# Top-k attention and two mixtures on one core: float64 weights converted by an integer sum, with raw words finished by the casts, later evictions of x, later products of w3, and exponentials written over the scores

## The chip, the core and the metric

One Trainium2 chip (trn2); the kernel runs on one of its cores. The metric is the device time of one execution in microseconds. The matrix engine is called PE (its weight loads PEld), the vector engine DVE, the scalar engine ACT, GpSimd POOL, and the engine that issues the transfers here SP. Each engine works through its own queue in order; an instruction that waits holds up all that stand behind it on the same engine.

## What is computed

Four batches of eight heads, 576 positions, 64 values per head. Each row of scores keeps its 32 largest and is normalised over them; the result x (2304 x 512) passes a first mixture, `(x w1 * x w2) w3 w_out`, and then a second one of eight experts with weights from a few rounds of normalising by rows and columns.

```python
scores = scale * np.matmul(q, k.transpose(0, 1, 3, 2))
kth = np.partition(scores, -top_k, axis=-1)[..., -top_k:-top_k + 1]
scores = np.where(scores >= kth, scores, -1000000000.0)
attn = np.exp(scores - np.max(scores, axis=-1, keepdims=True))
attn = attn / (np.sum(attn, axis=-1, keepdims=True) + 1e-09)
x = np.matmul(attn, v)
...
h = (x @ w1) * (x @ w2) @ w3
x = h @ w_out
...
out += P[:, e:e + 1] * (np.maximum(x @ w1[e], 0.0) @ w2[e])
```

The weights w1, w2, w3 and w_out of the first mixture arrive as float64, eight bytes per number, and the kernel makes float32 of them itself.

## The kernel before

**Attention steps.** The loop of line 615 runs once per step: a step treats two blocks of 128 score rows, and there are 72 steps (0 to 71) and a few more to empty the pipeline. In step s DVE finds the 32 largest of step s's rows (`st_topk`, lines 214 to 229: four rounds of MAX8 for two blocks, with three rounds of MATCH_REPLACE8 between them). In the same step ACT and POOL finish the rows of step s-1 (`st_over`, `st_bias`, `st_exp`: clamp, offset, exponential with its sum), DVE takes the reciprocal of step s-2's sums (`st_rec`, line 255) after its first MAX8, POOL normalises step s-2 (`st_norm`), PE transposes it (`st_trans`) and multiplies it with v (`st_av`), and PE makes the scores of step s+1 (`st_scores`), which ACT evicts. `st_av` ends with ACT's eviction of x (lines 295 and 304). Scores live in `s_sb` (three buffers), exponentials in `e_sb` (two).

**Conversions.** There are 40 pieces of 128x512 numbers (lines 399 to 420): 8 of w_out (key "o"), 16 of w3 (key "3"), 8 of w1, 8 of w2. `cv_run` (line 341) treats a piece in this way. From the top 16 bits of each raw word ACT makes two clamped numbers, `ca` and `cb` (lines 351 and 352). DVE joins them by a minimum and a maximum into the upper half of Q (line 359: the sign, the exponent and the first bits of the result as a float), masks sign and exponent out of Q (line 363) and multiplies the second word of the raw number by that power of two (line 373; for w_out ACT scales the word in line 356 and POOL multiplies in line 371). POOL adds the result to Q (lines 376 and 378). w1 and w2 are then split into a rounded upper part by ACT and a remainder by POOL (`hi_lo`, line 333). The DVE pieces are closures in `dve_q`; `st_topk` takes one after each pair of MAX8 and each pair of MATCH_REPLACE8, seven slots per step (`dve_slot`). `run_cv` is called twice in a step and starts the next piece while no more than three closures stand in the queue. The raw words have three buffers (`RB`), and the load for the piece three places on is issued behind the product (line 374).

**Work fed between.** While the attention steps run, PE is also given items from `fill` by a budget (`run_fill`, line 547). First come w3's transposes and its products with w_out (`w_items`, line 455), 5500 ns per step. When all of w3 is done, the conversion of w2 may begin (line 563, which closes the pools of w_out and w3); when w2 is converted, the first mixture starts (line 619). Its work for a batch has to be done by the step in which the next batch's attention ends (`marks`: steps 19, 37, 55, 73), and the budget of a step is what is left divided by the steps that are left (line 625).

Of the kernel before, what the change touches and what calls it, by code (L numbers as in the profile page):

```python
# [17 lines left out]
def kernel(  # L18
# [258 lines left out]
    def st_av(st):  # L277
# [6 lines left out]
        if steps1[st][0][1] is None:  # L284
# [8 lines left out]
            for j in range(2):  # L293
                b, hp = divmod(steps1[st][j][0], HP)
                nc.scalar.activation(xT[b][:, hp, S4:S], ps[:, 64 * j:64 * j + 64], AF.Copy)
            return
# [19 lines left out]
    gsc = G.rearrange("p f t -> p (f t)")  # L316
    cbias = const.tile([128, 2], F32, name="cbias")
    nc.gpsimd.memset(cbias[:, 0:1], -8.0 * 16 * 896)
    nc.gpsimd.memset(cbias[:, 1:2], -8.0 * (16 * 896 + 32768 - 4096))
    nc.gpsimd.memset(gsc[:, 0:2 * CW], 0.0)  # L320

    def cv_load(key, src):
        t = cv["p"].tile([128, 4 * CW + 4], U16, name="raw", tag="raw", bufs=RB)
# [17 lines left out]
    def cv_run(key, dst, done=None):  # L341
        t = raws.pop(key)
        pos = cpos[0]
        y = t[:, 4:4 * CW + 4].rearrange("p (n f) -> p n f", f=4)[:, :, 0]
        rest = t.bitcast(U32)[:, 0:2 * CW].rearrange("p (n f) -> p n f", f=2)[:, :, 1]
        n, m = cv["n"] % 2, cv["n"] % 3
        cv["n"] += 1
        Q = gsc[:, CW * n:CW * n + CW]
        ca = gsc[:, CW * (2 + m):CW * (3 + m)]
        cb = cv["p"].tile([128, CW], F32, name="cb", tag="cb", bufs=1 if "w2" in m1p else 2)  # L350
        nc.scalar.activation(ca, y, AF.Relu, bias=cbias[:, 0:1], scale=8.0)
        nc.scalar.activation(cb, y, AF.Identity, bias=cbias[:, 1:2], scale=8.0)

        off = key[0] == "o"
        if off:
            nc.scalar.activation(rest.bitcast(F32), rest, AF.Copy, scale=2.0 ** -36)

        def c1():
            nc.vector.scalar_tensor_tensor(Q.bitcast(U16).rearrange("p (n f) -> p n f", f=2)[:, :, 1],  # L359
                                           ca, 32768.0, cb, op0=ALU.min, op1=ALU.max)  # L360

        def c2():
            nc.vector.tensor_scalar(ca.bitcast(U32), Q.bitcast(U32), 0xff800000, None, op0=ALU.bitwise_and)

# [72 lines left out]
    def w_trans(i, hf):  # L437
        if hf == 0:
            w3t[i] = wtp.tile([128, FC, 128], F32, name="w3t", tag="w3t", bufs=1)
# [3 lines left out]
        nc.scalar.activation(w3t[i][:, 4 * hf:4 * hf + 4].rearrange("p a b -> p (a b)"), pt, AF.Copy)  # L443
        w3done.add((i, hf))
# [601 lines left out]
```

## Time and profile before

| | |
|---|---|
| median of three runs | 2446.41 us (2446.24 to 2447.53) |
| span of the profiled execution, first to last instruction | 2442.0 us |
| time of the profiled execution apart from its span | not stated by the profile |
| PE busy | 2288.3 us (94%) |
| DVE busy | 1958.9 us (80%) |
| POOL busy | 1343.2 us (55%) |
| ACT busy | 1256.2 us (51%) |
| attention steps 0 to 71, first MAX8 to last reciprocal | 14.25 to 806.1 us |

How to read it: the shares of a whole span mix stages. The attention steps fill the first third, the second mixture nearly all of the rest. An instruction's time on an engine can overlap the next one's start, so what a piece costs on an engine that never idles is the distance from its start to the next start, not its duration. A row such as "DVE rden L255 <- ACT rden L249: 8.0, 5, 4.1" says that DVE sat idle ahead of line 255 for 8.0 us in 5 cases, the longest 4.1, until ACT's line 249 was done.

### The profile page before, as it was taken

How to read it: one execution, taken by the hardware profiler on the slowest of the kernel's cores; microseconds unless marked ns; L12 is line 12 of the kernel's file. 1: busy time of each engine (PE TensorE's matmuls, PEld its weight loads, DVE VectorE, ACT ScalarE, POOL GpSimd, SP SyncE). 2: the span in 40 equal slices, each digit the busy share in tenths (PEclk: the TensorE clock that was granted, in tenths of full speed). 3: DMA queues.
4: the chain of work that ended last, by engine and by line, in shares of the span. 5: the costliest groups of instructions: out<-in, count | busy, mean ns of one | idle time of the engine just before them, and what ended most of it. 6: DMA issues, size and time to landing. Idle time of an engine off the chain costs nothing.

```text
span 2442.0 us, 37866 instructions
## 1 busy us (share of the span) xinstructions
PE 2288.3 (94%) x13061; PEld 2002.0 (82%) x13061; DVE 1958.9 (80%) x3560; ACT 1256.2 (51%) x2725; POOL 1343.2 (55%) x1377
## 2 busy tenths in 40 slices
PE   4677699899899999999999999999999999999999
PEld 3454489789788888889999988888888899999998
DVE  7998999999999228887777778777777777777776
ACT  6686777777777333444443444443444443444342
POOL 4534443233332125686666668666666666666664
PEclk7898789999999999999999999999999999999999
DMA  4332211111110132222222232222222322222221
GB/s 132 111 97 77 85 35 44 41 45 36 49 32 11 46 116 66 74 82 69 65 67 70 70 100 83 67 63 70 69 69 62 95 70 69 69 63 68 70 70 52
DMA packets 173296, 166.59 MB, mean 68 GB/s; under 512 B 19632, under 2 KB 137392, under 8 KB 173104
## 3 DMA queue, kind: packets, MB, share of 16 engines
q1 hardware_dynamic: 173104, 164.17, 22.4%
q8 instruction: 103, 1.69, 0.3%
q14 instruction: 89, 0.73, 0.1%
HBM read 145.24 MB, written 9.44 MB: 63 GB/s over the span
## 4 chain that ended last, share of the span: by engine, by line
PE 80%; DVE 11%; ACT 5%; POOL 2%; issue 2%; DMA 1%; SPq 0%; POOLq 0%; DVEq 0%; ACTq 0%
PE y L933 31%; PE l1ps L866 27%; PE abps L492 8%; PE x2ps L510 4%; DVE tkv L221 4%; DVE tk L227 3%; PE xps L300 3%; PE sps L198 2%; PE tps L267 2%; PE wps L451 1%; DVE G L359 1%; PE pt L137 1%; ACT e_sb L246 1%; ACT et L270 1%; ACT s_sb L202 1%
## 5 line engine op out<-in xcount | busy, mean ns | idle before, releaser
L730 POOL TENSOR_TENSOR wal<-ws,wah 128x256 fp32r<-128x256 f32 x665 | 553.9, 840 | 482.7 <-ACT wah L729 471.7
L946 DVE SCALAR_TENSOR_TENSOR acc<-y,P,acc 128x512 f32<-128x512 f32 x540 | 402.4, 745 | 215.0 <-PE y L933 214.0
L729 ACT ACTIVATE wah<-ws 128x256 fp32r<-128x256 f32 x672 | 276.3, 413 | 521.2 <-PE l1ps L866 514.9
L933 PE MATMUL y<-wbh,hh 128*128 128x512 f32 x1152 | 456.3, 396 | 4.5 <-ACT hh L887 4.5
L933 PE MATMUL y<-wbl,hh 128*128 128x512 f32 x1152 | 454.6, 395 | 0.0
L933 PE MATMUL y<-wbh,hl 128*128 128x512 f32 x1152 | 449.1, 390 | 1.9 <-DVE hl L890 1.4
L723 DVE TENSOR_TENSOR ws<-ws 128x256 f32<-128x256 f32 x384 | 319.0, 832 | 2.4 <-DMA ws<-in_moe_w_dram 1.8
L221 DVE MAX8 tkv<-tk 128x8 f32<-128x576 f32 x432 | 305.8, 752 | 0.0
L866 PE MATMUL l1ps<-xo0h,wah 128*128 128x384 f32 x896 | 304.6, 340 | 0.0
L866 PE MATMUL l1ps<-xo0h,wal 128*128 128x384 f32 x896 | 302.7, 338 | 0.0
L866 PE MATMUL l1ps<-xo0l,wah 128*128 128x384 f32 x896 | 302.7, 338 | 0.0
L933 PEld LDWEIGHTS y<-wbl,hh 128*128 128x128 f32 x1152 | 216.0, 188 | 52.7
L887 ACT ACTIVATE hh<-u 128x384 fp32r<-128x384 f32 x192 | 100.9, 525 | 297.0 <-DVE u L879 297.0
L933 PEld LDWEIGHTS y<-wbh,hl 128*128 128x128 f32 x1152 | 216.8, 188 | 30.3 <-DVE hl L890 5.8
L933 PEld LDWEIGHTS y<-wbh,hh 128*128 128x128 f32 x1152 | 216.6, 188 | 28.9 <-ACT hh L887 6.2
L738 POOL TENSOR_TENSOR wbl<-ws,wbh 128x1024 fp32r<-128x1024 f32 x96 | 231.8, 2414 | 12.5 <-ACT wbh L737 4.3
L227 DVE MATCH_REPLACE8 tk<-tkv,tk 128x576 f32<-128x576 f32 x288 | 212.4, 747 | 0.0
L866 PEld LDWEIGHTS l1ps<-xo0l,wah 128*128 128x128 f32 x896 | 169.2, 189 | 16.3
L866 PEld LDWEIGHTS l1ps<-xo0h,wah 128*128 128x128 f32 x896 | 168.9, 189 | 16.0 <-DVE hl L890 0.9
L501 POOL TENSOR_TENSOR G<-a_sb 128x256 f32<-128x256 f32 (+1 forms) x64 | 52.3, 817 | 227.4 <-ACT a_sb L497 211.6
L866 PEld LDWEIGHTS l1ps<-xo0h,wal 128*128 128x128 f32 x896 | 168.7, 188 | 0.0
L879 DVE TENSOR_TENSOR u<-l1ps,u 128x384 f32<-128x384 f32 x288 | 157.2, 546 | 4.8 <-PE l1ps L866 3.0
(146 smaller groups left out, 4912.2 us busy)
## 6 DMA issues: line engine op xcount, KB each, us to landing
ws<-in_moe_w_dram SPq DMA_DIRECT2D x384, 128.0 KB, 2.3
ws<-in_moe_w_dram SPq DMA_DIRECT2D x96, 512.0 KB, 3.5
raw<-in_moe_w_dram SPq DMA_DIRECT2D x32, 512.0 KB, 3.7
kst<-kst SPq DMA_DIRECT2D x30, 288.0 KB, 4.0
xr<-x2s SPq DMA_DIRECT2D x12, 384.0 KB, 3.6
xr<-x2s SPq DMA_DIRECT2D x6, 768.0 KB, 4.7
kn<-in_k_dram SPq DMA_DIRECT2D x16, 256.0 KB, 2.7
qn<-in_q_dram SPq DMA_DIRECT2D x16, 256.0 KB, 2.8
```

Of the source, the lines that this page charges most:

```text
L221: nc.vector.max(vt[:, j, 8 * r:8 * r + 8], a[j] if r else s[j])
L227: nc.vector.match_replace(a[j], vt[:, j, 8 * r:8 * r + 8], a[j] if r else s[j], -3.0e38)
L492: nc.tensor.matmul(ps[:, 0:n], lhs[:, c, fs], rhs[:, c, 0:n], start=(c == 0 and j == 0), stop=(c == KD - 1 and j == 2))
L723: nc.vector.tensor_tensor(st[:, dst], st[:, x], st[:, y], op)
L729: nc.scalar.activation(hi, st[:, slot], AF.Copy)
L730: eng.tensor_tensor(lo, st[:, slot], hi.bitcast(F32), ALU.subtract)
L738: nc.gpsimd.tensor_tensor(lo, st, hi.bitcast(F32), ALU.subtract)
L866: nc.tensor.matmul(ps[:, 0:TH], lhs[:, c], rhs[:, slot, c], start=(k_ == 0), stop=(k_ == 3 * KH - 1))
L879: nc.vector.tensor_tensor(t[nm], ps, t[x], ALU.add)
L887: nc.scalar.activation(t["hh"][:, i, h], src, AF.Relu)
L933: nc.tensor.matmul(ps, lhs[:, m, h, o:o + 128], rhs[:, m], start=(k_ == 0), stop=(k_ == 5))
L946: nc.vector.scalar_tensor_tensor(a, ps, P[:, t, e:e + 1], a, op0=ALU.mult, op1=ALU.add)
```

## The change

Five things are changed, all ahead of the second mixture.

- **Conversion.** ACT now scales the second raw word for every piece, not for w_out alone, and writes it as a 32-bit integer (`low`). The mask and the product go, on DVE and on POOL. POOL's sum adds Q and `low` as integers. `cb` is a Copy with a constant instead of an Identity with a bias tile. A piece still takes three slots, of which two are empty and the last holds the minimum and maximum.
- **Raw words end with the casts.** Nothing reads the raw buffer after ACT's three casts, the load for the piece two places on is issued right behind them, and there are two raw buffers.
- **x is evicted a step later.** The eviction of `st_av`'s result is issued in the next step, behind the first exponential.
- **w3's products a step later.** A half of w3 is transposed, and the four products issued with it are those of the half before; `w3t` is kept by halves in two buffers.
- **Exponentials overwrite the scores.** `e_sb` is the tile `s_sb`, now with four buffers. The 1e-9 is added to the sums by DVE (line 253 of the changed kernel), ahead of the reciprocal, and no longer by ACT (line 249 before). `cv_flush` is called ahead of the step's first `run_cv`.

```diff
@@ -198,7 +197,7 @@
-            s_sb[st] = ap1.tile([128, 2, S], F32, name="s_sb", tag="s_sb", bufs=3)
+            s_sb[st] = ap1.tile([128, 2, S], F32, name="s_sb", tag="s_sb", bufs=4)
...
     def st_exp(st, j):
         if j == 0:
-            e_sb[st] = ap1.tile([128, 2, S], F32, name="e_sb", tag="e_sb", bufs=2)
+            e_sb[st] = s_sb[st]
...
         if j:
-            nc.scalar.activation(rd, rd, AF.Identity, bias=eps)
             nbias.pop(st)
             s_sb.pop(st)
 
     def st_rec(st):
         rd = rden[st]
+        nc.vector.tensor_scalar(rd, rd, 1e-9, None, op0=ALU.add)
         nc.vector.reciprocal(rd, rd)
...
-        nc.scalar.activation(xT[b][:, hp, 128 * t:128 * t + 128], ps[:, 0:128], AF.Copy)
+        xev.append(lambda: nc.scalar.activation(xT[b][:, hp, 128 * t:128 * t + 128], ps[:, 0:128], AF.Copy))
+
+    xev = []
+
+    def st_out():
+        while xev:
+            xev.pop(0)()
...
-    RB = 3
+    RB = 2
...
-    def cv_next(n):
-        if n < len(cvs) and not n - 3 < NCA <= n:
+    def cv_next(pos):
+        n = pos + RB
+        if n < len(cvs) and not pos < NCA <= n:
             cvs[n][1]()
...
-        nc.scalar.activation(ca, y, AF.Relu, bias=cbias[:, 0:1], scale=8.0)
-        nc.scalar.activation(cb, y, AF.Identity, bias=cbias[:, 1:2], scale=8.0)
-
-        off = key[0] == "o"
-        if off:
-            nc.scalar.activation(rest.bitcast(F32), rest, AF.Copy, scale=2.0 ** -36)
+        ca = gsc[:, CW * (2 + n):CW * (3 + n)]
+        cb = cv["p"].tile([128, CW], F32, name="cb", tag="cb", bufs=2)
+        low = (cv["p"].tile([128, CW], F32, name="lw", tag="lw", bufs=1) if n else gsc[:, 4 * CW:5 * CW]).bitcast(I32)
+        nc.scalar.activation(ca, y, AF.Relu, bias=cbias, scale=8.0)
+        nc.scalar.activation(cb, y, AF.Copy, bias=-8.0 * (16 * 896 + 32768 - 4096), scale=8.0)
+        nc.scalar.activation(low, rest, AF.Copy, scale=2.0 ** -13)
+        cv_next(pos)
+
+        def split():
+            hi_lo(low.bitcast(F32), *dst())
 
         def c1():
             nc.vector.scalar_tensor_tensor(Q.bitcast(U16).rearrange("p (n f) -> p n f", f=2)[:, :, 1],
                                            ca, 32768.0, cb, op0=ALU.min, op1=ALU.max)
-
-        def c2():
-            nc.vector.tensor_scalar(ca.bitcast(U32), Q.bitcast(U32), 0xff800000, None, op0=ALU.bitwise_and)
...
-        def c3():
-            if off:
-                nc.gpsimd.tensor_tensor(ca, rest.bitcast(F32), ca, ALU.mult)
+            if key[0] in ("o", "3"):
+                nc.gpsimd.tensor_tensor(dst().bitcast(I32), Q.bitcast(I32), low, ALU.add)
             else:
-                nc.vector.scalar_tensor_tensor(ca, rest, 2.0 ** -36, ca, op0=ALU.mult, op1=ALU.mult)
-            cv_next(pos + 3)
-            if key[0] in ("o", "3"):
-                nc.gpsimd.tensor_tensor(dst(), Q, ca, ALU.add)
-            else:
-                nc.gpsimd.tensor_tensor(ca, Q, ca, ALU.add)
-                cv_post.append(lambda: hi_lo(ca, *dst()))
+                nc.gpsimd.tensor_tensor(low, Q.bitcast(I32), low, ALU.add)
+                cv_post.append(split)
             if done is not None:
                 done()
 
-        dve_q.extend([c1, c23] if off else [c1, c2, c3])
+        dve_q.extend([None, None, c1])
...
+    w_last = []
+
     def w_items(i, hf):
-        return [(430, lambda: w_trans(i, hf))] + [(860, lambda j=j: w_mm(i, j)) for j in range(4 * hf, 4 * hf + 4)]
+        r = [(430, lambda: w_trans(i, hf))] + w_last
+        w_last[:] = [(860, lambda j=j: w_mm(i, j)) for j in range(4 * hf, 4 * hf + 4)]
+        if (i, hf) == (FC - 1, 1):
+            r += w_last
+        return r
...
         if new:
             st_exp(s - 1, 0)
+        st_out()
...
+        cv_flush()
         if 0 < s and cpos[0] < len(cvs):
             run_cv()
-        cv_flush()
```

The order in which the instructions stand on the engines, at three places. On DVE, the end of a step with two conversions and the beginning of the next (MAX on `tk` are the last rounds, MAX on `s_sb` the next step's first), before:

```order
L359 SCALAR_TENSOR_TENSOR G<-G,cb 128x512
L221 MAX tkv<-tk_769 128x8
L221 MAX tkv<-tk_770 128x8
L363 TENSOR_SCALAR G<-G 128x512
L227 MATCH_REPLACE tk_769<-tkv,tk_769 128x576
L227 MATCH_REPLACE tk_770<-tkv,tk_770 128x576
L373 SCALAR_TENSOR_TENSOR G<-raw,G 128x512
L221 MAX tkv<-tk_769 128x8
L221 MAX tkv<-tk_770 128x8
L221 MAX tkv<-s_sb 128x8
L255 RECIPROCAL rden<-rden 128x2
```

and with the change:

```order
L226 MATCH_REPLACE tk_745<-tkv,tk_745 128x576
L226 MATCH_REPLACE tk_746<-tkv,tk_746 128x576
L220 MAX tkv<-tk_745 128x8
L220 MAX tkv<-tk_746 128x8
L226 MATCH_REPLACE tk_745<-tkv,tk_745 128x576
L226 MATCH_REPLACE tk_746<-tkv,tk_746 128x576
L368 SCALAR_TENSOR_TENSOR G<-G,cb 128x512
L220 MAX tkv<-tk_745 128x8
L220 MAX tkv<-tk_746 128x8
L220 MAX tkv<-s_sb 128x8
L253 TENSOR_SCALAR rden<-rden 128x2
L254 RECIPROCAL rden<-rden 128x2
```

The mask and the product of each piece are gone, the minimum and maximum (line 368 now) stands where the product stood, and an addition (line 253) stands between the first MAX of the step and the reciprocal.

On ACT, from the casts of a step's first piece into the next step, before:

```order
L270 ACTIVATE et<-tps 128x640
L351 ACTIVATE G<-raw,cbias 128x512
L352 ACTIVATE cb<-raw,cbias 128x512
L126 ACTIVATE qhl<-qn 128x9x64
L443 ACTIVATE w3t<-pt 128x512
L304 ACTIVATE xT<-xps 128x128
L453 ACTIVATE W<-wps 128x512
L351 ACTIVATE G<-raw,cbias 128x512
L352 ACTIVATE cb<-raw,cbias 128x512
L234 ACTIVATE s_sb<-s_sb,tkv 128x576 x2
L202 ACTIVATE s_sb<-sps 128x576
```

and with the change:

```order
L359 ACTIVATE G<-raw,cbias 128x512
L360 ACTIVATE cb<-raw 128x512
L361 ACTIVATE lw<-raw 128x512
L127 ACTIVATE qhl<-qn 128x9x64
L437 ACTIVATE w3t<-pt 128x512
L359 ACTIVATE G<-raw,cbias 128x512
L360 ACTIVATE cb<-raw 128x512
L361 ACTIVATE G<-raw 128x512
L233 ACTIVATE s_sb<-s_sb,tkv 128x576 x2
L201 ACTIVATE s_sb<-sps 128x576
L245 ACTIVATE s_sb,rden<-s_sb,nbias 128x576
L304 ACTIVATE xT<-xps 128x128
```

Each piece has a third cast (line 361, written to `lw` or a part of G), and the eviction of x (line 304) has moved from between the two pieces' casts to behind the next step's first exponential.

On PE, the first half of w3 that is transposed (`pt<-ident,w3r`) and what follows it, before:

```order
L442 MATMUL pt<-ident,w3r 128x128 x4
L451 MATMUL wps<-wo,w3t 128x512 x2
L267 MATMUL tps<-ident,e_sb 128x128 x4
L268 MATMUL tps<-ident,e_sb 128x128
L198 MATMUL sps<-kst_311,qst_94 128x288 x2
L198 MATMUL sps<-kst_334,qst_94 128x288 x2
L267 MATMUL tps<-ident,e_sb 128x128 x4
L268 MATMUL tps<-ident,e_sb 128x128
L451 MATMUL wps<-wo,w3t 128x512 x2
L300 MATMUL xps<-et,vn_91 64x128 x10
```

and with the change:

```order
L436 MATMUL pt<-ident,w3r 128x128 x4
L266 MATMUL tps<-ident,s_sb 128x128 x4
L267 MATMUL tps<-ident,s_sb 128x128
L197 MATMUL sps<-kst_300,qst_94 128x288 x2
L197 MATMUL sps<-kst_325,qst_94 128x288 x2
L266 MATMUL tps<-ident,s_sb 128x128 x4
L267 MATMUL tps<-ident,s_sb 128x128
L300 MATMUL xps<-et,vn_91 64x128 x10
L197 MATMUL sps<-kst_300,qst_94 128x288 x2
L197 MATMUL sps<-kst_325,qst_94 128x288 x2
L138 MATMUL pt<-ident,qhl 128x128 x4
L436 MATMUL pt<-ident,w3r 128x128 x4
```

Before, products (`wps`) of the half just transposed follow at once; now no product follows until the next half has been transposed (the last row); the first product (line 445) stands right behind that row. Further on, the first product of the first mixture (`abps`) follows 42 transposed blocks of exponentials before and 44 with the change: one step more.

## Rows read from the trace of the kernel before

**Rows 1.** The page: its first line, and the chain that ended last by engine.

```profile
span 2442.0 us, 37866 instructions
...
PE 80%; DVE 11%; ACT 5%; POOL 2%; issue 2%; DMA 1%; SPq 0%; POOLq 0%; DVEq 0%; ACTq 0%
```

**Rows 2.** Busy time by stretch: from:to, length, each engine, clock, DMA share, GB/s.

```profile
core 0: us, PE busy (x) PEld busy (x) DVE busy (x) ACT busy (x) POOL busy (x), PEclk, DMA share, GB/s
14.25:42.34 28.09, 10.54 (x38) 7.80 (x38) 23.19 (x48) 18.01 (x34) 11.24 (x10) 0.55 0.52 166
42.34:78.30 35.96, 21.69 (x140) 18.15 (x140) 35.96 (x78) 31.78 (x62) 24.27 (x22) 0.78 0.37 118
78.30:249.31 171.01, 130.15 (x731) 82.15 (x732) 157.80 (x322) 120.86 (x242) 69.61 (x71) 0.89 0.30 94
249.31:323.35 74.04, 45.55 (x249) 35.80 (x245) 74.04 (x152) 54.99 (x109) 39.35 (x40) 0.64 0.22 64
323.35:462.87 139.52, 138.92 (x1141) 126.07 (x1141) 136.97 (x296) 106.50 (x240) 46.78 (x65) 1.00 0.16 43
462.87:801.79 338.92, 316.98 (x2574) 281.35 (x2573) 338.92 (x735) 255.21 (x565) 109.70 (x152) 0.98 0.12 34
```

**Rows 3.** Groups on DVE, 0 to 860 us: count, busy us, mean ns, idle before.

```profile
L359 DVE SCALAR_TENSOR_TENSOR G<-G,cb 128x512 uint16<-128x512 f32 x40 | 34.9, 873 | 12.2 <-ACT cb L352 12.2
...
L373 DVE SCALAR_TENSOR_TENSOR G<-raw,G 128x512 f32<-128x512 uint32 x32 | 21.9, 684 | 0.0
...
L363 DVE TENSOR_SCALAR G<-G 128x512 uint32<-128x512 uint32 x40 | 18.8, 471 | 0.0
```

**Rows 4.** DVE in order of time in step 11: start, duration, instruction.

```profile
164.84 0.42 DVE L363 TENSOR_SCALAR G<-G 128x512 uint32<-128x512 uint32 x1
165.17 1.42 DVE L221 MAX8 tkv<-tk 128x8 f32<-128x576 f32 x2
166.50 0.68 DVE L373 SCALAR_TENSOR_TENSOR G<-raw,G 128x512 f32<-128x512 uint32 x1
167.09 0.09 DVE L227 MATCH_VALUE_LOAD tk<-tkv,tk 128x8 f32 x1
```

**Rows 5.** Busy time of single steps: with two conversions, and with nothing fed in.

```profile
149.00:162.04 13.04, 13.04 (x92) 8.92 (x91) 13.04 (x28) 11.25 (x23) 4.96 (x5) 1.00 0.47 124
...
472.57:482.27 9.70, 5.16 (x45) 4.15 (x47) 9.70 (x22) 7.63 (x17) 4.02 (x4) 0.95 0.10 30
```

**Rows 6.** Lines 255 and 839 (shortest/median/longest ns), and dependent DVE instructions in time.

```profile
L255 DVE RECIPROCAL rden<-rden x72: 133/152/181, 42.3 to 806.1; 128x2 f32<-128x2 f32 x72
...
L839 DVE TENSOR_SCALAR cs<-cs x8: 172/374/2047, 940.9 to 997.2; 128x8 f32<-128x8 f32 x8
...
949.43 0.20 DVE L840 RECIPROCAL cs<-cs 128x8 f32<-128x8 f32 x1
949.67 0.42 DVE L841 TENSOR_SCALAR cs<-cs 128x8 f32<-128x8 f32 x1
```

**Rows 7.** DVE and POOL in order of time at step 40's reciprocal.

```profile
491.98 0.14 DVE L255 RECIPROCAL rden<-rden 128x2 f32<-128x2 f32 x1
...
491.90 0.73 POOL L501 TENSOR_TENSOR G<-a_sb 128x256 f32<-128x256 f32 x1
```

**Rows 8.** Waits in 78.30 to 249.31: us in total, times, longest us.

```profile
PE wps L451 <- ACT w3t L443: 38.9, 13, 7.0
...
ACT xT L304 <- PE xps L300: 19.0, 8, 6.1
...
DVE G L359 <- ACT cb L352: 9.0, 5, 2.6
```

**Rows 9.** Groups on ACT, 20 to 805 us.

```profile
L249 ACT ACTIVATE rden<-rden,eps 128x2 f32<-128x2 f32 x71 | 21.0, 296 | 2.3
...
L356 ACT ACTIVATE raw<-raw 128x512 f32<-128x512 uint32 x7 | 4.7, 672 | 0.0
```

**Rows 10.** Line 376 on POOL: shortest/median/longest ns.

```profile
L376 POOL TENSOR_TENSOR w3r<-G x16: 1267/1276/1286, 75.0 to 215.7; 128x512 f32<-128x512 f32 x16
```

More of the change, by code (lines that the diff above doesn't have):

```diff
@@ L11 @@
 U32 = mybir.dt.uint32
+I32 = mybir.dt.int32
 AF = mybir.ActivationFunctionType
@@ L182 @@
     tkv, nbias, rden = {}, {}, {}
-    eps = const.tile([128, 1], F32, name="eps")
-    nc.gpsimd.memset(eps, 1e-9)
     def st_scores(st, j):
@@ L294, in st_av @@
                 b, hp = divmod(steps1[st][j][0], HP)
-                nc.scalar.activation(xT[b][:, hp, S4:S], ps[:, 64 * j:64 * j + 64], AF.Copy)
+                xev.append(lambda b=b, hp=hp, j=j: nc.scalar.activation(xT[b][:, hp, S4:S], ps[:, 64 * j:64 * j + 64],
+                                                                        AF.Copy))
             return
@@ L316 @@
     gsc = G.rearrange("p f t -> p (f t)")
-    cbias = const.tile([128, 2], F32, name="cbias")
-    nc.gpsimd.memset(cbias[:, 0:1], -8.0 * 16 * 896)
-    nc.gpsimd.memset(cbias[:, 1:2], -8.0 * (16 * 896 + 32768 - 4096))
+    cbias = const.tile([128, 1], F32, name="cbias")
+    nc.gpsimd.memset(cbias, -8.0 * 16 * 896)
     nc.gpsimd.memset(gsc[:, 0:2 * CW], 0.0)
     def cv_load(key, src):
-        t = cv["p"].tile([128, 4 * CW + 4], U16, name="raw", tag="raw", bufs=RB)
+        t = cv["p"].tile([128, 4 * CW + 4], U16, name="raw", tag="raw",
+                         bufs=RB)
         nc.sync.dma_start(t[:, 1:4 * CW + 1], src.bitcast(U16))
         raws[key] = t
-    def cv_next(n):
-        if n < len(cvs) and not n - 3 < NCA <= n:
+    def cv_next(pos):
+        n = pos + RB
+        if n < len(cvs) and not pos < NCA <= n:
             cvs[n][1]()
@@ L345, in cv_run @@
         rest = t.bitcast(U32)[:, 0:2 * CW].rearrange("p (n f) -> p n f", f=2)[:, :, 1]
-        n, m = cv["n"] % 2, cv["n"] % 3
+        n = cv["n"] % 2
         cv["n"] += 1
         Q = gsc[:, CW * n:CW * n + CW]
-        ca = gsc[:, CW * (2 + m):CW * (3 + m)]
-        cb = cv["p"].tile([128, CW], F32, name="cb", tag="cb", bufs=1 if "w2" in m1p else 2)
-        nc.scalar.activation(ca, y, AF.Relu, bias=cbias[:, 0:1], scale=8.0)
-        nc.scalar.activation(cb, y, AF.Identity, bias=cbias[:, 1:2], scale=8.0)
-        off = key[0] == "o"
-        if off:
-            nc.scalar.activation(rest.bitcast(F32), rest, AF.Copy, scale=2.0 ** -36)
+        ca = gsc[:, CW * (2 + n):CW * (3 + n)]
[7 more added lines that the diff above has]
+            hi_lo(low.bitcast(F32), *dst())
         def c1():
@@ L437, in w_trans @@
     def w_trans(i, hf):
-        if hf == 0:
-            w3t[i] = wtp.tile([128, FC, 128], F32, name="w3t", tag="w3t", bufs=1)
+        w3t[i, hf] = wtp.tile([128, 4, 128], F32, name="w3t", tag="w3t", bufs=2)
         pt = mps.tile([128, 512], F32, name="pt", tag="mm")
@@ L442, in w_trans @@
             nc.tensor.transpose(pt[:, 128 * j:128 * j + 128], w3r[i, hf][:, 128 * j:128 * j + 128], ident)
-        nc.scalar.activation(w3t[i][:, 4 * hf:4 * hf + 4].rearrange("p a b -> p (a b)"), pt, AF.Copy)
+        nc.scalar.activation(w3t[i, hf].rearrange("p a b -> p (a b)"), pt, AF.Copy)
         w3done.add((i, hf))
@@ L450, in w_mm @@
             wps[i] = mps.tile([128, 512], F32, name="wps", tag="mm")
-        nc.tensor.matmul(wps[i], w3t[i][:, j], wo[:, j], start=(j == 0), stop=(j == FC - 1))
+        nc.tensor.matmul(wps[i], w3t[i, j // 4][:, j % 4], wo[:, j], start=(j == 0), stop=(j == FC - 1))
         if j == FC - 1:
             nc.scalar.activation(W[:, i], wps.pop(i), AF.Copy)
+    w_last = []
     def w_items(i, hf):
-        return [(430, lambda: w_trans(i, hf))] + [(860, lambda j=j: w_mm(i, j)) for j in range(4 * hf, 4 * hf + 4)]
+        r = [(430, lambda: w_trans(i, hf))] + w_last
[3 more added lines that the diff above has]
+        return r
     def moe1_pool():
@@ L557, in run_cv @@
         n = cpos[0]
-        if n >= len(cvs) or sum(f is not None for f in dve_q) > 3:
+        if n >= len(cvs) or len(dve_q) > 3:
             return
@@ L563, in run_cv @@
         if n == NCA and "w2" not in m1p:
-            if dve_q or cv_post or fill or later_q or (FC - 1, 1) not in w3done:
+            if any(dve_q) or cv_post or fill or later_q or (FC - 1, 1) not in w3done:
                 return
             wt_close()
-            for i in range(3):
+            for i in range(RB):
                 cvs[n + i][1]()
@@ L578 @@
     cvs[0][1]()
-    nc.scalar.activation(eps, eps, AF.Copy)
+    nc.scalar.activation(cbias, cbias, AF.Copy)
     prep_split(0, "k", nc.vector)
@@ L591 @@
     cvs[1][1]()
-    cvs[2][1]()
     load_v(1)
@@ L618 @@
         now[0] = s
-        if s >= marks[0] and "p" not in m1p and cpos[0] == len(cvs) and not dve_q and not cv_post:
+        if s >= marks[0] and "p" not in m1p and cpos[0] == len(cvs) and not any(dve_q) and not cv_post:
             moe1_pool()
```

3 lines of the change are left out of this document (removed).

## The prediction

> **What bounds the kernel now.** I read the chain of waits first: PE holds 80% of it [rows 1]. That share is made late, where the second mixture keeps PE full and where the change touches nothing; so I cut the span by stages, at the reciprocal of line 255, which DVE runs once per attention step, 0.65 us into it [rows 2]. The reader is to see that DVE is busy for all of four of these stretches: steps 2 to 4 (42.34 to 78.30), 17 to 22 (249.31 to 323.35) and 37 to 71 (462.87 to 801.79) without a gap, steps 5 to 16 (78.30 to 249.31) with 13.2 us of gaps in 171.01, and the first two steps with 4.9 in 28.09. The stretch 323.35 to 462.87 (steps 23 to 36) is the exception: DVE has gaps of 2.6 us and PE is busy for 138.92 of 139.52 at full clock. So DVE sets the pace wherever conversions run, and PE sets it while the first batch of the first mixture is fed in. After 801.79 PE works alone.
>
> A step without conversions takes DVE 9.70 us, and PE then needs 5.2 [rows 5]. The three DVE pieces of a conversion are line 359 (min/max), 363 (mask), 373 (product) [rows 3]. Instructions overlap, so I count from start to start: the mask takes 165.17 - 164.84 = 0.33 us, the product 167.09 - 166.50 = 0.59 [rows 4]. A step with two conversions and no gap took 13.04 [rows 5], which leaves (13.04 - 9.70) / 2 - 0.33 - 0.59 = 0.75 for the min/max. Counted in DVE's timeline, the 40 masks and 32 products fall into the first four stretches of [rows 2] as 3 and 0, 6 and 1, 23 and 23, 8 and 8.
>
> **The change, part by part.** *Masks and products go, one addition comes.* A one-operand addition on 128x2 is added before each reciprocal. The nearest rows are additions and products on 128x8 further on (line 839): 0.17 us at the shortest [rows 6]. It cannot overlap with the reciprocal, which reads its result; between two such dependent instructions lies 949.67 - 949.43 - 0.20 = 0.04 us. I take 0.20 per step. A gain is excluded, since nothing leaves DVE for it; the upper end is another one of the same rows, 2.05 us.
>
> *What that addition may wait for.* Line 839 runs from 172 to 2047 ns for the same eight elements, while the two-element reciprocal of line 255 stays between 133 and 181 ns [rows 6]. So this form is held by something that does not hold the reciprocal. In steps 37 to 71, eleven of 35 reciprocals began while a POOL instruction was in progress, the first 0.08 us into one of 0.73 us [rows 7]; what was left of these eleven adds up to 5.2 us in the two timelines, and in steps 2 to 22 to about 9. If all are waited for, steps 37 to 71 pay 35 x 0.20 + 5.2 = 12.2 us; if none, 7.0. I take 9.5, since each DVE step becomes longer and POOL is likelier to be done. The Trainium skill (SBUF — State Buffer, "Who interferes with whom") says that a one-tensor operation like this can enter a mode that uses the port pair shared with GpSimd, and that whoever comes second then blocks fully. By that rule the sum would take the 12.2, without it the 7.0; it speaks against this part of the change. The trace agrees as far as the spread of L839 shows it.
>
> *Steps 0 and 1.* Three masks go (1.0 us). The min/max now stands two slots later in the queue; the 3.2 us that DVE waited for line 352 there go (12.2 in all [rows 3], of which 9.0 lie in steps 5 to 16 [rows 8]). -4 us; ends 0 and -4.9, all gaps.
>
> *Steps 2 to 4.* Six masks and a product (-2.6), three additions (+0.6), some of it given back in waits for POOL: -1.5, ends 0 and -2.
>
> *Steps 5 to 16.* Work on DVE falls from 12 x 9.70 + 23 x 1.67 = 154.8 (busy for 157.8) to 12 x 9.90 + 23 x 0.75 = 136, plus 1 for additions that wait: 137, 11.4 per step. Now the neighbours. PE is busy for 130.15 in this stretch, 10.8 per step. ACT is busy for 120.86; it loses 12 additions of 0.30 us and gains 21 casts of 0.67 (the words' lower parts; only w_out's had one before) [rows 9], so 131.4, 10.9 per step. Three engines within 5% of one another, handing work round, will not run without gaps. What made the gaps is taken away: DVE waited 9.0 us for line 352; behind that ACT sat 19.0 us before xT's eviction (now issued half a step later, so its product is ready) and PE 38.9 before w3's products (now a step behind their transposes) [rows 8]. The ends are 137 (no gaps) and 150 (all 13.2 stay). I take 145, nearer to the upper end because ACT and PE are closer to full than before. -26 us, ends -34 and -21.
>
> *Steps 17 to 22.* Work 6 x 9.90 + 8 x 0.75 = 65.4 against 74.04. w2's lower halves are subtracted on POOL just when the step's addition falls due, and ACT's casts now stand behind w2's eviction, which waits for POOL's sum; I add 5 for both. -4, ends 0 and -8.6.
>
> *Steps 23 to 36: dearer.* w3's last products come a step later, so line 564's test passes in step 17 and not 16, and the first mixture starts in step 23 and not 22 (on PE its first product follows 44 transposed blocks instead of 42, two to a step). Its first batch, 76.8 us by the code's own costs, is due by step 37: thirteen steps instead of fourteen. PE's 138.92 less 14 x 5.2 leaves 66.1 of feeding; over 13 steps that is 5.1 + 5.2 = 10.3 per step, more than DVE's 9.90. 9.9 + 13 x 10.3 = 143.8, with a little waiting 144.5: +5. Here the addition on DVE costs nothing, PE's longer step covers it; without that cover 14 x 0.2 = 2.8. Ends +2.8 and +8.
>
> *Steps 37 to 71*: +9.5, ends +7 and +12.2.
>
> *At nothing:* exponentials over the scores (same shapes; a fourth score buffer replaces two others, and the old one's last reader, PE's transposes, is done a step before); the moved flush; two raw buffers instead of three (a load is now issued after the casts, and has a step until its use); ACT's saved 0.30 per step after step 22, where ACT is busy 255 of 339. POOL's sum was a float add of 1.28 us [rows 10], and is now one of 32-bit integers; DVE does not wait for it, so I cost it at nothing as long as POOL, busy 69.6 of 171 in steps 5 to 16, has room. After 801.79: +0.3 for the last xT.
>
> Sum: -4 - 1.5 - 26 - 4 + 5 + 9.5 + 0.3 = -20.7. The profiled span of 2442.0 becomes 2421.3. The median of the runs shown lies 4.4 us above that span (the profile states no other time of its own); carried over: 2426 us.
>
> **The rivals.** (A) *DVE runs at its floor*: no gaps in steps 5 to 16 (-34 instead of -26), few port waits. For: every wait that caused a gap is addressed. Against: ACT at 10.9 of 11.4. Time 2418, at the very best (all lower ends) about 2406. (B) *ACT or PE becomes the bound* of steps 5 to 16: 13 us per step as before, 156 in all, -15: 2437. For: the added casts; against: a step in which PE was busy throughout and ACT for 11.25 ran without a gap on DVE [rows 5]. (C) *The addition waits for POOL in most steps*: with L839's median of 0.37 in place of 0.17, 56 steps outside 23 to 36 pay 0.2 more each: 2426 + 11 = 2437, less what is already counted, 2433. (D) *Slower: the integer sum is slow on POOL.* No row shows one. POOL's step in steps 5 to 16 then needs two sums and about 3 us of other work (normalising, splits). At 1.28 it has room; at 5.6 us a sum the step is 14.2 us, as long as before, and with steps 23 to 71 at +14.5 the kernel is at 2446 - 5 + 14.5 = 2455; from there on every us of a sum costs some 30. It decides from about 5 us on, over four times the float add. (E) B and C together use up the gain: about 2446, no change.
>
> **How the numbers follow.** Forecast (2418 to 2433) 0.48; A, below 2418, 0.17; B 0.14; C, where it is above 2433, 0.08; E 0.07; D 0.06. No change means within 0.2%, 4.9 us, about what a measurement of this kernel can tell. Faster takes the forecast, A, B and a third of C: 0.82. Same takes E and the rest of C: 0.12. Slower is D: 0.06. The range runs from 2408 (below it only the last of A, 0.05) to 2444 (above it D and most of E, 0.13).
>
> **What would show it.** Right: reciprocals 9.9 us apart in steps 37 to 71 and 10.3 apart in 24 to 36, about 12 in steps 5 to 16; line 451's products no longer waiting for ACT; the additions of line 253 mostly at 0.17 with a few up to 1 us. Wrong: steps of 13 with DVE idle behind ACT (B); additions of 0.4 and more in the mean (C); POOL sums of several us (D); a step of 9.7 in 37 to 71 would mean the addition is hidden, and the time 7 lower.

## The result and the profile after

| | before | changed |
|---|---|---|
| median of the runs of this comparison | 2446.32 us (2444.89 to 2447.53) | 2419.73 us (2418.34 to 2420.30) |
| ratio | | 0.9895, 95% interval 0.9881 to 0.9909 |
| span of the profiled execution | 2442.0 us | 2416.5 us |
| DVE busy | 1958.9 us | 1937.9 us |
| PE, ACT, POOL busy | 2288.3, 1256.2, 1343.2 us | 2292.5, 1247.4, 1326.1 us |

The change saves 26.6 us, 1.1%; 20 were forecast, and 2419.73 lies in the range. Several terms of the sum missed in opposite directions, so part of that agreement is luck; the runs below take them apart.

The page of the changed kernel, its span and the chain that ended last:

```profile
span 2416.5 us, 37811 instructions
...
PE 74%; DVE 16%; ACT 4%; issue 2%; POOL 2%; DMA 1%; SPq 0%; POOLq 0%; ACTq 0%; DVEq 0%
```

Busy time of the changed kernel by the stretches of [rows 2], cut at its reciprocals (line 254 now); the columns are those of [rows 2]:

```profile
14.25:38.44 24.19, 10.55 (x38) 8.14 (x38) 22.15 (x45) 16.77 (x33) 6.97 (x7) 0.55 0.59 171
38.44:72.72 34.28, 22.42 (x140) 18.43 (x140) 34.18 (x72) 31.03 (x60) 15.33 (x17) 0.77 0.44 131
72.72:211.21 138.49, 120.39 (x712) 76.73 (x711) 138.07 (x288) 127.07 (x254) 65.01 (x71) 0.93 0.34 106
211.21:279.26 68.05, 46.04 (x292) 36.31 (x291) 67.84 (x141) 57.33 (x113) 35.71 (x39) 0.75 0.30 93
279.26:420.42 141.16, 137.99 (x1114) 124.77 (x1113) 138.89 (x309) 99.40 (x223) 49.47 (x67) 0.99 0.15 40
420.42:770.21 349.79, 323.22 (x2578) 285.86 (x2577) 348.49 (x769) 243.90 (x532) 110.33 (x152) 0.96 0.12 33
```

The third row is the gain: steps 5 to 16 take 138.49 us instead of 171.01, and DVE is busy for all but 0.4 of them, where it had 13.2 us of gaps. The last row is the price in the later steps, 349.79 instead of 338.92. What follows the end of the last row (the reciprocal that opens step 72; one more comes 4 us later) takes 2416.5 - 770.21 = 1646.3 us, against 2442.0 - 801.79 = 1640.2: 6 us more, nearly all of it in the second mixture, of which no line is touched.

The changed kernel's groups on DVE, 0 to 860 us, against [rows 3]; the second row is the new addition:

```profile
L368 DVE SCALAR_TENSOR_TENSOR G<-G,cb 128x512 uint16<-128x512 f32 x40 | 30.2, 754 | 0.0
L253 DVE TENSOR_SCALAR rden<-rden 128x2 f32<-128x2 f32 x72 | 23.5, 327 | 5.2 <-ACT s_sb L245 5.2
...
L254 DVE RECIPROCAL rden<-rden 128x2 f32<-128x2 f32 x72 | 11.9, 166 | 2.5
```

The minimum and maximum no longer waits for `cb` (12.2 us of idle time before, 0.0 now). The addition takes 327 ns in the mean. Its durations, shortest, median and longest, stand in the row of line 253 alone:

```profile
L253 DVE TENSOR_SCALAR rden<-rden x72: 146/157/1368, 38.2 to 774.1; 128x2 f32<-128x2 f32 x72
```

Half of them take 0.157 us or less, and the mean is made by a few long ones. One of these in the changed kernel's timeline (start, duration, instruction):

```profile
668.49 2.95 POOL L476 TENSOR_TENSOR xl<-xT,xh 128x1280 fp32r<-128x1280 f32 x1
...
670.17 1.30 DVE L253 TENSOR_SCALAR rden<-rden 128x2 f32<-128x2 f32 x1
...
671.39 0.20 POOL L238 TENSOR_TENSOR nbias<-tkv 128x2 f32<-128x2 f32 x1
671.50 0.17 DVE L254 RECIPROCAL rden<-rden 128x2 f32<-128x2 f32 x1
```

POOL's subtraction ends at 668.49 + 2.95 = 671.44, the addition at 671.47. The reciprocal behind it starts while POOL runs line 238 and still takes 0.17. Of the 72 additions, 20 began while a POOL instruction was in progress. Three of these took under 0.2 us, with at most 0.17 us of POOL's instruction left; the other 17 are all the additions that took over 0.2 us, and each ended 0.02 to 0.03 us after POOL's instruction. Above the median the 17 waited 12.2 us together. Twenty reciprocals began during a POOL instruction, which in 11 cases ran on for 0.6 to 2.9 us, and none was held. The Trainium skill (SBUF — State Buffer, "Who interferes with whom") calls the port pair that DVE and GpSimd share an exclusive lock; these 17 agree with it, the longest at 1.37 us for two elements.

### The profile page after: what moved, and what is told of

It reads as the page before. It is cut to its first block, busy times and chain, and to the rows that moved or that the text cites. A ratio compares the mean times of both kernels' runs of the same rounds, so it can differ in the third digit from the quotient of the medians.

```text
span 2416.5 us, 37811 instructions
## 1 busy us (share of the span) xinstructions
PE 2292.5 (95%) x13061; PEld 2005.3 (83%) x13061; DVE 1937.9 (80%) x3560; ACT 1247.4 (52%) x2685; POOL 1326.1 (55%) x1367
## 3 DMA queue, kind: packets, MB, share of 16 engines
q1 hardware_dynamic: 173104, 164.17, 22.8%
## 4 chain that ended last, share of the span: by engine, by line
PE 74%; DVE 16%; ACT 4%; issue 2%; POOL 2%; DMA 1%; SPq 0%; POOLq 0%; ACTq 0%; DVEq 0%
PE y L933 32%; PE l1ps L866 28%; DVE tkv L220 7%; DVE tk L226 6%; PE abps L492 6%; PE x2ps L510 3%; PE xps L300 1%; PE sps L197 1%; PE tps L266 1%; DVE G L368 1%; ACT s_sb L245 1%; ACT et L269 1%; PE pt L138 1%; ACT s_sb L201 0%; DVE rden L253 0%
## 5 line engine op out<-in xcount | busy, mean ns | idle before, releaser
L933 PE MATMUL y<-wbh,hl 128*128 128x512 f32 x1152 | 455.5, 395 | 0.4
```

The source lines that it names most:

```text
L933: nc.tensor.matmul(ps, lhs[:, m, h, o:o + 128], rhs[:, m], start=(k_ == 0), stop=(k_ == 5))
```

## The experiments

Each comparison below has 7 to 13 runs of the kernel before (medians 2446.3 to 2447.5) on the same chip.

### Why the second mixture became slower

The change drops the tile `eps`, and with it the tiles allocated behind it on the left side of the on-chip memory move down, by 32 bytes in each partition; the right side does not move. No trace states an address. That the step is 32 bytes is borne out by the runs below: 32 unused bytes, and elsewhere the tile `eps` itself, bring back the same 312.80 us for the units compared here.

The second mixture runs in units, 32 for each third s = 0, 1, 2 of the positions. In a unit PE multiplies x (for s = 1 the left tiles xo1h and xo1l, otherwise tiles on the right) with an expert's first weights, and in line 933 of the changed kernel the result (hh and hl) with the second weights (wbh and wbl, made of ws2); acc collects the sums. First the old places are restored:

```diff
     gsc = G.rearrange("p f t -> p (f t)")
+    pad = const.tile([128, 8], F32, name="pad")
+    nc.gpsimd.memset(pad, 0.0)
```

> The changed kernel with 32 unused bytes per partition put back among the constants, so that every tile allocated from the left (hh, hl, wbh, wbl, acc, xo1) lies at the address it had before the change. Theory 'place': the second mixture's units take 15.73 us in the changed kernel where they took 15.64 before, only because these tiles lie 32 bytes lower; with the bytes back they take 15.64 again (15.72 in the middle third), the second mixture is 5 to 6 us shorter, and the kernel takes 2414. Rival 'history': PE's pace depends on how it was used before; the units stay at 15.73 and the kernel at 2420. The attention steps stay as in the changed kernel under both.

Measured: 2413.9 us (2412.72 to 2414.60), ratio 0.9864 (0.9849 to 0.9879). ACT writes `wbh` once in each of the 96 units. Twenty units at s = 2, from one such row to the twentieth after it, in the timeline of the kernel before, then of the changed one, then with 32 unused bytes:

```profile
2029.28 1.04 ACT L737 ACTIVATE wbh<-ws 128x1024 fp32r<-128x1024 f32 x1
...
2342.08 1.04 ACT L737 ACTIVATE wbh<-ws 128x1024 fp32r<-128x1024 f32 x1
```

```profile
2001.39 1.05 ACT L737 ACTIVATE wbh<-ws 128x1024 fp32r<-128x1024 f32 x1
...
2316.05 1.05 ACT L737 ACTIVATE wbh<-ws 128x1024 fp32r<-128x1024 f32 x1
```

```profile
1999.88 1.04 ACT L739 ACTIVATE wbh<-ws 128x1024 fp32r<-128x1024 f32 x1
...
2312.68 1.04 ACT L739 ACTIVATE wbh<-ws 128x1024 fp32r<-128x1024 f32 x1
```

312.80, 314.66 and 312.80 us. With PE busy throughout and at full clock, the same products take 0.09 us more per unit, and 32 unused bytes give it back. Over the whole stage behind step 71, the profiled executions of five kernels with these tiles at their old places (the one before, this one, and three from further on) take 1640.1 to 1643.0 us, those of five with the tiles 32 bytes lower 1646.2 to 1649.0. So the 6 us of this stage belong to the tiles' places; in the profile of this run 3.4 of them come back, and by the medians the kernel is 5.8 us faster. Three more runs ask which tiles. 64 unused bytes instead of 32:

> The changed kernel with 64 unused bytes instead of 32, so that the left tiles lie 32 bytes above their places of before instead of 32 below. Theory 'what counts is whether the tiles start on a multiple of 64 bytes': they don't, so units of 15.73 us and 2419.5 us (2417.5 to 2421.5) as for the changed kernel. Rival 'any place not below that of before will do': units of 15.64 us, 2414 us.

32 bytes ahead of hh alone (behind xo1h, xo1l, acc and ws2):

```diff
     w2_load(0, 0)
+    pad = wp.tile([128, 8], F32, name="pad")
+    nc.gpsimd.memset(pad, 0.0)
```

> The changed kernel with 32 unused bytes ahead of the tiles hh: hh, hl, wbh and wbl (the operands of line 933's products) start on multiples of 64 bytes, the inputs xo1h, xo1l and the sum acc stay 32 off. Theory 'the operands of line 933's products are the cause': units of the first and last third at 15.64 us, about 2414.5 us (2413 to 2416). Rival 'acc, read and written by DVE, is the cause': 15.73 us, 2419.5 us.

and the same tile created behind hl, just ahead of wbh:

> The changed kernel with 32 unused bytes between hl and wbh: only the weights wbh and wbl start on multiples of 64 bytes, hh and hl stay 32 off. Theory 'hh and hl, which the products stream, are the cause': units stay at 15.73 us, 2419.5 us (2417.5 to 2421.5). Rival 'the loaded weights are the cause': 15.64 us, 2414 us.

Measured, with the distance of the tiles from their places of before, which by the sizes of the tiles ahead of them are multiples of 64 bytes, counted from where the left side starts:

| kernel | xo1, acc, ws2 | hh, hl | wbh, wbl | 20 units, s = 1 | 20 units, s = 2 | time (us) |
|---|---|---|---|---|---|---|
| before | 0 | 0 | 0 | 314.40 | 312.80 | |
| changed | -32 | -32 | -32 | 314.93 | 314.66 | 2419.73 |
| 32 bytes | 0 | 0 | 0 | 314.40 | 312.80 | 2413.90 |
| 64 bytes | +32 | +32 | +32 | 314.13 | 313.47 | 2415.62 |
| ahead of hh | -32 | 0 | 0 | 311.60 | 312.80 | 2409.59 |
| ahead of wbh | -32 | -32 | 0 | 315.47 | 314.20 | 2418.34 |

Two of these rows at s = 1, from the timeline with 32 unused bytes and then from that with the bytes ahead of hh:

```profile
1497.35 1.04 ACT L739 ACTIVATE wbh<-ws 128x1024 fp32r<-128x1024 f32 x1
...
1811.75 1.04 ACT L739 ACTIVATE wbh<-ws 128x1024 fp32r<-128x1024 f32 x1
```

```profile
1495.30 1.05 ACT L737 ACTIVATE wbh<-ws 128x1024 fp32r<-128x1024 f32 x1
...
1806.90 1.05 ACT L737 ACTIVATE wbh<-ws 128x1024 fp32r<-128x1024 f32 x1
```

The intervals of the last three ratios are 0.9856 to 0.9885, 0.9834 to 0.9863, 0.9865 to 0.9898. `acc` and `ws2` are out as the cause: with both 32 bytes off, s = 2 runs at 312.80. At s = 2 it is mostly hh and hl (and the small tiles between them and wbh, which move with them); putting wbh and wbl alone back gives 0.5 of the 1.9 us. The plain rule that I had expected, a start on a multiple of 64 bytes, falls twice: 32 bytes above is better than 32 below, and at s = 1, where PE reads xo1h and xo1l, the unit is shortest with these 32 bytes off: 311.60 instead of 314.40, which is why the kernel's 2409.59 lies below the range of either theory. Nor is it the distance of the left tiles from one another alone: in the first four rows of the table it is the same, and s = 2 runs at three paces. What in the memory makes it so stays open.

### What the addition costs, and where

```diff
         rd = rden[st]
-        nc.vector.tensor_scalar(rd, rd, 1e-9, None, op0=ALU.add)
         nc.vector.reciprocal(rd, rd)
```

> The changed kernel without the addition of 1e-9 to the softmax sums (left out altogether; a sum holds the row's largest term, exp(0) = 1, so a float32 sum is the same with and without it). Theory: the addition is on DVE's path; the reciprocals of steps 37 to 71 come 9.70 apart instead of 9.90 (-7 us) and the waits behind POOL instructions go (12 us in the changed kernel's trace, of which some 10 on the path), less what ACT and PE then set in steps 5 to 16 and 24 to 36: 2397, between 2394 and 2403. Rival: the waits only stand in for others (the normalising on POOL, PE in the first mixture), and at most 7 us come off: 2412 or more.

Measured: 2400.79 us (2400.21 to 2401.83), ratio 0.9811 (0.9797 to 0.9826). The addition costs 18.9 us: steps 37 to 71 fall from 349.79 to 340.93, steps 5 to 16 from 138.49 to 132.50, steps 17 to 22 from 68.05 to 63.18; only steps 23 to 36 become longer (144.45), and there DVE idles for 6.9 us instead of 2.3 while PE is busy for 141.0. With the 32 bytes as well:

> The changed kernel without the addition of 1e-9 (left out of the computation) and with 32 unused bytes that put the left tiles back at their places of before. Theory 'the two costs are separate': 2400.8 - 5.8 = 2395 (2393 to 2397), units of the second mixture at 15.64/15.72/15.64 us. Rival 'the one covers part of the other': 2398 to 2401.

Measured: 2394.26 us (2392.99 to 2396.32), ratio 0.9784 (0.9769 to 0.9799): the two costs are separate. And with the addition where it was, on ACT:

```diff
+    eps = const.tile([128, 1], F32, name="eps")
+    nc.gpsimd.memset(eps, 1e-9)
...
         if j:
+            nc.scalar.activation(rd, rd, AF.Identity, bias=eps)
             nbias.pop(st)
...
-        nc.vector.tensor_scalar(rd, rd, 1e-9, None, op0=ALU.add)
```

> The changed kernel with the addition of 1e-9 left on ACT as before (with its constant tile, which puts the left tiles back at their places of before). Theory 'the addition costs because it stands on DVE, at the bound, behind POOL': ACT has room, so about 2396 (2394 to 2400), steps 37 to 71 at 9.70 us, and this beats both kernels. Rival 'on ACT it delays the reciprocal or ACT's casts by as much as it costs on DVE': 2408 to 2414.

Measured: 2397.85 us (2396.58 to 2399.16), ratio 0.9798 (0.9783 to 0.9813). With the tiles in the same places, the addition costs 2413.9 - 2394.26 = 19.6 us on DVE and 3.6 on ACT. Steps 37 to 71 take 342.52 us here, and in them DVE's reciprocal hardly waits for ACT's addition:

```profile
L256 DVE RECIPROCAL rden<-rden 128x2 f32<-128x2 f32 x36 | 5.5, 153 | 0.4 <-ACT rden L250 0.3
```

### What took the gaps out of steps 5 to 16

Three parts of the change were to do it. First w3's products back behind their own transposes, all else as changed:

```diff
-        r = [(430, lambda: w_trans(i, hf))] + w_last
-        w_last[:] = [(860, lambda j=j: w_mm(i, j)) for j in range(4 * hf, 4 * hf + 4)]
-        if (i, hf) == (FC - 1, 1):
-            r += w_last
-        return r
+        return [(430, lambda: w_trans(i, hf))] + [(860, lambda j=j: w_mm(i, j)) for j in range(4 * hf, 4 * hf + 4)]
```

> The changed kernel with w3's products issued right behind their own half's transposes, as before the change (w3t stays in two halves). Theory 'waits': the later products are one of the two things that took DVE's 13 us of gaps out of steps 5 to 16; PE waits some 35 to 40 us for the eviction of the transposes again, steps 5 to 16 grow from 138.5 to 145 to 151, the first mixture starts one step earlier (-2.5): 2424 to 2430. Rival 'slots': the gaps went because the minimum and maximum stands two slots later and has half a step more; PE's waits come back, DVE has no gaps, and the kernel takes 2417 (the earlier start alone).

Measured: 2449.48 us (2447.03 to 2452.57), ratio 1.0012 (1.0002 to 1.0022): the whole gain is gone, more than any theory had expected. Steps 5 to 16 take 170.12 us, and DVE is idle for 33.0 of them. Three of the waits of that stretch:

```profile
PE wps L445 <- ACT w3t L437: 36.8, 14, 4.8
...
DVE rden L253 <- ACT s_sb L245: 19.3, 7, 5.8
ACT W L447 <- PE wps L445: 16.6, 3, 8.1
```

Then x evicted at once, with `st_out()` called right behind each product of `st_av`, all else as changed:

> The changed kernel with x evicted directly behind its products, as before the change. Theory 'waits': ACT sits for PE's x products again (19 us in steps 5 to 16 before) while it is busy for 10.6 of 11.5 us in a step, so DVE gets gaps of 5 to 10 us there, and steps 24 to 31 of the first mixture, 9.91 apart in the changed kernel, go back above 10: 2426 to 2434. Rival 'slots': there is slack enough; ACT waits, DVE does not, and the kernel takes 2420, plus at most 2 for the first mixture.

Measured: 2419.85 us (2419.33 to 2421.12), ratio 0.9890 (0.9875 to 0.9904): no difference. In steps 5 to 16 ACT waits for the product of x

```profile
ACT xT L305 <- PE xps L301: 1.3, 3, 0.7
```

where the kernel before waited 19.0 us [rows 8]: that wait was not due to the eviction's place but to PE, which stood before w3's products with x's product behind them. Next, the new conversion alone, on the kernel before:

```diff
-    RB = 3
+    RB = 2
...
+        nc.scalar.activation(low, rest, AF.Copy, scale=2.0 ** -13)
...
-        dve_q.extend([c1, c23] if off else [c1, c2, c3])
+        dve_q.extend([None, None, c1])
...
+        cv_flush()
         if 0 < s and cpos[0] < len(cvs):
             run_cv()
-        cv_flush()
```

> The kernel before with the new conversion alone (integer sum, casts, two raw buffers, the flush ahead of the conversion): w3's products right behind their own transposes, x evicted at once, own tiles for the exponentials, the 1e-9 added by ACT, and with it the tiles of the kernel before at their places. Theory 'the masks and products alone are the gain': DVE loses 0.92 us per conversion and keeps no gaps, about 2410 us (2402 to 2416), steps 5 to 16 within 140. Theory 'the gain needs w3's products a step later': gaps of some 30 us in steps 5 to 16 as in the run with w3's products at once; that run's 2449.5 less the addition's 19 and the tiles' 5.5 is about 2425 (2418 to 2432), steps 5 to 16 at 155 to 170.

Measured: 2428.81 us (2427.71 to 2429.84), ratio 0.9924 (0.9910 to 0.9939). The time is in the second theory's range, steps 5 to 16 are 3 us above theirs. The gain lies in steps 0 to 4 (56.9 us from the first MAX8 on, instead of 64.1) and 17 to 22 (64.06 instead of 74.04). In steps 5 to 16 there is none at all:

```profile
71.49:244.71 173.22, 130.28 (x716) 80.76 (x714) 135.04 (x276) 129.59 (x262) 65.65 (x69) 0.88 0.30 92
```

DVE's work falls from 157.80 to 135.04, about what the prediction had counted (12 x 9.70 + 23 x 0.75 = 133.7; its 136 has the additions), and its gaps grow from 13.2 to 38.2. One of them in this kernel's timeline:

```profile
108.14 0.60 PE L432 MATMUL pt<-ident,w3r 128*128 128x128 f32 x4
...
110.10 0.77 ACT L354 ACTIVATE G<-raw,cbias 128x512 f32<-128x512 uint16 x1
...
112.43 0.60 ACT L433 ACTIVATE w3t<-pt 128x512 f32<-128x512 f32 x1
...
113.08 3.65 PE L441 MATMUL wps<-wo,w3t 128*128 128x512 f32 x4 [4.34 <-ACT w3t L433]
...
116.66 1.31 PE L301 MATMUL xps<-et,vn 128*64 128x128 f32 x20
116.71 0.74 DVE L228 MATCH_REPLACE8 tk<-tkv,tk 128x576 f32<-128x576 f32 x1
117.90 1.98 PE L441 MATMUL wps<-wo,w3t 128*128 128x512 f32 x4
118.02 0.28 ACT L305 ACTIVATE xT<-xps 128x128 f32<-128x128 f32 x1 [4.99 <-PE xps L301]
119.92 0.60 ACT L443 ACTIVATE W<-wps 128x512 f32<-128x512 f32 x1 [1.63 <-PE wps L441]
120.42 0.77 ACT L354 ACTIVATE G<-raw,cbias 128x512 f32<-128x512 uint16 x1
...
121.09 0.64 ACT L355 ACTIVATE cb<-raw 128x512 f32<-128x512 uint16 x1
...
121.83 0.74 DVE L363 SCALAR_TENSOR_TENSOR G<-G,cb 128x512 uint16<-128x512 f32 x1 [4.38 <-ACT cb L355]
```

It is a ring. The transposes of w3 (`pt`) are done at 108.74, but ACT runs a piece's casts (from 110.10 on) ahead of their eviction to `w3t`. PE waits 4.34 us for it, then needs 3.65 for four products (the granted clock from 112.90 to 116.60, after that wait, was 0.54, near the lower of its levels, 1.2 GHz; the four from 117.90 on took 1.98) and only then gets to x's product; ACT waits 4.99 us for that with the next casts queued behind it; DVE waits 4.38 us for the casts. Less work on DVE left the length as it was here, and the gaps took the place of the work. Last, the other way round, the changed kernel with the old conversion:

```diff
-    RB = 2
+    RB = 3
...
-        dve_q.extend([None, None, c1])
+        dve_q.extend([c1, c23] if off else [c1, c2, c3])
```

> The changed kernel with the old conversion (mask and product on DVE, the float sum, three raw buffers); everything else as changed. Theory 'DVE's work sets the pace and the moved products only close gaps': the time before (2446.3) plus 19 for the addition on DVE and 5.5 for the tiles' places, less up to 13 for gaps closed: 2450 to 2462, steps 5 to 16 near 160. Theory 'the moved products are the gain and the conversion is not': 2415 to 2430.

Measured: 2459.31 us (2458.47 to 2459.99), ratio 1.0048 (1.0031 to 1.0065). Steps 5 to 16:

```profile
80.67:242.84 162.17, 134.09 (x739) 86.98 (x740) 161.76 (x333) 119.57 (x234) 72.92 (x73) 0.85 0.31 91
```

The gaps are gone here too (0.4 us), and DVE's own work is the whole length. So the four lengths of steps 5 to 16 are

| | products at once | products a step later |
|---|---|---|
| old conversion | 171.0 | 162.2 |
| new conversion | 173.2 | 138.5 |

(the right column with the addition on DVE, which costs 6.0 of the 138.5 by the run without it). The columns differ in the rest of the change too: on the right, exponentials are written over the scores and x is evicted later. With all of that and the products at once, the new conversion took 170.1 (the first run of this section), so there the products alone are worth 31.6. For the old conversion no run moves the products alone, and none moves them without the exponentials over the scores; what the 162.2 owes to each stays open. Alone the conversion gives nothing and the rest of the change 9; together they give 32.5: the one takes away work of DVE, the other its gaps.

### All of it together

The addition on ACT, its constant in a second column of `cbias`, so that no tile moves, and 32 bytes ahead of hh:

```diff
+            nc.scalar.activation(rd, rd, AF.Identity, bias=cbias[:, 1:2])
...
-        nc.vector.tensor_scalar(rd, rd, 1e-9, None, op0=ALU.add)
...
-    cbias = const.tile([128, 1], F32, name="cbias")
...
+    cbias = const.tile([128, 2], F32, name="cbias")
...
+    nc.gpsimd.memset(cbias[:, 1:2], 1e-9)
...
+    pad = wp.tile([128, 8], F32, name="pad")
```

> The changed kernel with the addition of 1e-9 on ACT as before (its constant in a second column of the tile cbias, so that no tile moves for it) and 32 unused bytes ahead of hh as in the run with hh padded. It computes everything. Theory 'the addition's place and the tiles' places are separate costs that add up': 2397.85 less the 4.3 us that the padded hh had gained over the run with all left tiles put back: 2393.5 us (2391.5 to 2395.5), units of the second mixture at 15.64/15.58/15.64 us, steps 37 to 71 within 344 us. Rival 'the 4.3 us belong to a pattern that the addition on ACT changes': 2396 to 2399.

Measured: 2393.70 us (2392.52 to 2395.78), ratio 0.9779 (0.9763 to 0.9796), with everything computed: 26 us below the changed kernel, 53 below the one before.

## Why the prediction was right, and where it was wrong

The right reason was that DVE sets the pace and that work taken off it shows wherever it has no gaps before and after. By the terms of the sum, in us (the profiled executions):

| stretch | forecast | measured | |
|---|---|---|---|
| steps 0 and 1 | -4 | -3.9 | right |
| steps 2 to 4 | -1.5 | -1.7 | right |
| steps 5 to 16 | -26 | -32.5 | in its ends (-34 and -21), at the far one |
| steps 17 to 22 | -4 | -6.0 | in its ends |
| steps 23 to 36 | +5 | +1.6 | below its lower end of +2.8 |
| steps 37 to 71 | +9.5 | +10.9 | right |
| after step 71 | +0.3 | +6.1 | not foreseen |
| sum | -20.7 | -25.5 | |

- **Steps 5 to 16.** The step that failed is "three engines within 5% of one another, handing work round, will not run without gaps". DVE did run without them, busy for all but 0.4 of 138.5 us, and the three were not that close: PE was busy for 120 where 130 had been carried over, ACT for 127 where 131 were counted. Once PE no longer waits for `w3t`, the ring is open. The cause was named in part: the later products do it, the later eviction of x does nothing. A sum of work and gaps also suggests that the lighter conversion alone earns its share of the 26; in its run DVE's work fell by 22.8 us and the stretch grew by 2.2. The waits for POOL were mis-sized as well: 1 us was counted, and six additions waited 4.5.
- **Steps 23 to 36.** "10.3 per step", over thirteen steps, was mis-sized. The first mixture's first product comes 8.5 us into step 23 (at 287.79), but before the change it came 2.8 us into the same step (at 326.12), so the delay is less than the whole step that the sum had taken. And only the last six steps took 10.30 in the mean (9.90 to 11.39), as two windows of the changed kernel show:

```profile
299.11:358.60 59.49, 58.67 (x470) 54.46 (x470) 59.28 (x133) 43.51 (x99) 22.16 (x29) 1.00 0.13 36
358.60:420.42 61.82, 61.82 (x484) 54.54 (x484) 59.83 (x133) 42.94 (x97) 20.06 (x29) 1.00 0.15 44
```

  In the first, six steps at 9.91, DVE is busy but for 0.2 us and PE has 0.8 us to spare; in the second PE has none. I had spread the feeding evenly.
- **Steps 37 to 71.** Right, with its mechanism: most steps take 9.90 to 9.92 instead of 9.70, the 0.20 that was forecast. Six additions waited there, 3.4 us in all; I had taken 2.5. The reciprocal had met POOL in eleven of these steps, the addition in seven; in six of them it was held to POOL's end, in the seventh 0.06 us of POOL's instruction was left. (For steps 2 to 22 the prediction gives about 9 us as what was left of POOL's instructions; the timeline has 8.1.)
- **After step 71.** "Where the change touches nothing" was wrong: it moved the tiles' addresses, which no view of the kernel before shows. That is the +6.
- **The rivals.** A (no gaps in steps 5 to 16, few port waits) came true in its first half, and the 12.2 us of waits speak against its second. B (ACT or PE as the bound) is refuted by the 0.4 us of gaps. C would have needed a median of 0.37 us; it is 0.157. D: the integer sum takes 1.27 to 1.29 us for 128x512, as the float one did [rows 10]. Two things offset one another, and that is luck: steps 5 to 16 gave 6.5 more than forecast, the addresses took 5.8.

## What to carry to other kernels

Where two limits hold the same stretch, taking one away alone can give little or nothing: here -9 (with an added operation on DVE in it) and +2 us, against -32.5 together. So test such parts in pairs, and look at the stretch, not at the total. An operation of 0.16 us on the engine that sets the pace cost 20 us over 72 steps, much of it waits for another engine; on an engine with room it cost 4, although it takes 0.30 us there. When a change adds or drops a tile, compare the addresses of the operands in the hot loop, even of one that is not touched.

## What the runs showed of the hardware

- With PE busy throughout at full clock, shifts of 32 bytes of the tiles that hold its operands changed the pace by up to 1.2%: 311.60 to 315.47 us for the same 20 units at s = 1, 312.80 to 314.66 at s = 2.
- A 128x2 addition on DVE that began during a POOL instruction ended with it (17 cases, up to 1.37 us; in the run with x evicted at once one that began 6 ns after POOL's instruction was not held, 0.15 us); a 128x2 reciprocal was not held (0.17 us each, in 11 cases with 0.6 to 2.9 us of POOL's instruction left).
- POOL added 32-bit integers at the rate of floats: 1.27 to 1.29 us for 128x512 in the rows of the new conversion, 1.27 to 1.29 before [rows 10].
